# A new order of steps and new shares of casts in the first batch of an attention-and-ReGLU kernel

## The chip, the cores and the metric

The kernel runs on one core of one Trainium2 chip. The metric is the device time of one execution in microseconds (us). The kernel before took 243.38 us (median of 3 runs, 243.06 to 243.96).

## What is computed

Four batches of 12,416 rows of width 128 go through two attention steps against 32 inducing vectors, and the result goes through a ReGLU block of hidden width 1536. Cut to what matters:

```python
def mab(q, kv):
    s = scale * (q @ kv.transpose(0, 2, 1))
    s = s - s.max(-1, keepdims=True)
    a = np.exp(s)
    a /= a.sum(-1, keepdims=True) + 1e-09
    return a @ kv
h = mab(I, x)            # 32 x 128 for each batch, from all 12416 rows of x
y = mab(x, h)            # 12416 x 128 for each batch
gate = np.maximum(y @ w_gate, 0.0)
out = (gate * (y @ w_val)) @ w_out     # 49664 x 128
```

Only 32 values of attention stand between `h` and the output, so that the ReGLU of a row is a quadratic form in these 32 weights; the kernel turns the weights `w_gate`, `w_val` and `w_out` together with `h` into small tables for each batch (the "tables" below) and never forms the 1536-wide product for a row.

## The kernel before

The work of a batch has two stages. The first makes `h`: x is cast to fp16, transposed, multiplied with the inducing vectors (scores), the exponential is taken, and sums over all rows are collected in PSUM. The second makes the gates and tables from `h`, and then the outputs of the batch in blocks of 16 tiles of 128 rows. The second stage of batch 0 and all of batches 1 to 3 stand in one interleaved program that a long text, `ORDER`, spells out step by step. It is not touched.

The first stage of batch 0 has a function of its own, `first_batch`, in which the order is a text too, `HEAD`. The 97 tiles of 128 rows of the batch come in 16 parts, numbered 0 to 15: parts 0 to 9 have 8 tiles each except part 3, which is the one tile left over; parts 10 to 15 have 4 tiles. One DMA for each part is issued on SP (L288), the parts in their order, into four fp32 buffers (parts 0 to 2, 4 to 6, 7 to 9 and 10 to 15), and after them the two weight matrices (L330, L331). A word in `HEAD` is a letter for a step and the number of a part:

- `P`, `A`, `D`: cast of a share of the part's tiles from fp32 to fp16, on POOL, ACT and DVE (L374). `SHARES` says how many tiles each of the three engines takes. The tiles of a part go to POOL first, then to ACT, then to DVE.
- `t`: transposes on PE, one for each tile, into a PSUM bank (L384); `c`: copy of the bank to `xT` on DVE (L388).
- `s`: scores on PE (L394); `e`: exponential on ACT (L400); `h`: the sums on PE (L410 or L421 for the denominators, L425 for the numerators).
- `r0`: a reduction on DVE of the denominators of all 8-tile parts; it is added in front of the last part's sums (L419).

Each engine executes its own words strictly in the order of the text, so a word that is placed early in `HEAD` and has to wait holds up all that follows on its engine. Scores and transposes share a ring of three PSUM banks (tag `g`), in the order of the text too; the exponentials share four buffers.

Behind the last word, POOL casts `w_gate` (L445), issues the load of `w_out` (L446) and the loads of batch 1's x, which cast to fp16 on the way (`x16q`, L236, six of 16 tiles and one of the tile left over). ACT casts `w_val` (L447). PE runs three idle matmuls (`idle`, L357: their result is not read). DVE takes the reciprocal of the denominators (L452), makes `h` (L454) and its centred copies (`centre`, L245 to L266).

`ORDER` begins there: PE makes the gates (L881) and the first scores of the second stage (L511), DVE reads the gates (`gm`, L895, and what follows it), ACT takes the exponential `p` (L520). The buffers of this stage lie where the buffers of the first stage were, so `gm` waits, beside the gates, for the casts of both weights. Two further places matter below: the transposes of batch 1's x on PE (L763), which wait for the `x16q` loads, and the differences on PE (L567), which feed ACT and DVE. Some idle matmuls stand in `ORDER` as well (L1179).

The first stage has further idle matmuls (L357): one in front of the transposes of part 1 and one in front of those of part 2, and three in front of those of part 12, the thirteenth part.

Of the kernel before, what the change touches and what calls it, by code (L numbers as in the profile page):

```python
# [16 lines left out]
class Plan:  # L17
# [68 lines left out]
    (4, 4, 0),  # L86
    (4, 4, 0),
    (4, 4, 0),
    (2, 2, 0),
    (0, 2, 2),  # L90
    (2, 1, 1),
    (2, 2, 0),
    (1, 1, 2),
    (2, 2, 0),
]
HEAD = """
A0 P0 t0 P1 c0 A1 t1 P2 c1 D3 P4 A2 s0 t2 P5 P6 c2 e0 t3 A4 s1 c3 h0 s3 e1 s2 h1 A5 t4 P7 e3 e2
t5 h2 A6 A7 c4 s4 P8 h3 P9 t6 c5 t7 e4 s5 A8 h4 P10 c6 e5 c7 s6 s7 e6 t8 A9 h5 t9 e7 A10 t10
P12 c8 c9 c10 D11 s8 h6 e8 h7 s10 D12 A11 e10 s9 A12 P13 t11 c11 h8 P14 e9 t12 s11 A13 c12 e11
h10 t13 D14 s12 h11 c13 P15 A14 t14 h9 c14 e12 s13 r0 A15 t15 e13 s14 c15 e14 h12 h13 s15 h14  # L100
e15 h15"""

ORDER = """
Ov00LQ0Lu4OV4M24LG4Ow2Oy25k0La000050Or04Oz03Lk0P0020U0Mw0A+0MC0Ox2011Os2Ou2Ot2O-106001000u0524s0P42
# [63 lines left out]
def square_body(ctx, tc, x, inducing, moe_w_gate, moe_w_val, moe_w_out, out):  # L168
# [99 lines left out]
    def first_batch(sp, psum):  # L268
        def bank(tag, name, shape=None, dtype=FP32):
            return psum.tile(  # L270
                shape or [P, BLK], dtype, tag=tag, bufs={"g": 3, "v": 2, "o": 1}[tag], name=name
            )
# [48 lines left out]
        xT = {q: xTq[q] if q < NQ else xTr[0] for q in range(NQ + 1)}  # L321
        hT_ps = bank("o", "hT_ps", [P, M])
        z1a_ps = bank("v", "z1a_ps", [P, 2 * BLK])
        z1a, idle_ps = z1a_ps[:, 0 : 8 * M], z1a_ps[:, BLK : 2 * BLK]
# [28 lines left out]
        n_big = sum(t1 - t0 in (8, 1) for t0, t1 in parts)  # L353

        def idle(ps, n, rhs):
            for _ in range(n):
                nc.tensor.matmul(ps[:, 0 : rhs.shape[-1]], eye16, rhs, start=True, stop=True)  # L357

        def turn(j):
            t0, t1 = parts[j]  # L360
            ps = bank("g", "xT_ps", [P, 8, P], FP16)
            for t in range(t0, t1):
                nc.tensor.transpose(ps[:, t - t0, :], x16[:, t, :], eye16)
            nc.vector.tensor_copy(out=xTs(xT, t0, t1 - t0), in_=ps[:, 0 : t1 - t0, :])

        def part(j):
            return (*parts[j], x32s[j], x16[:, parts[j][0] : parts[j][1], :])
# [8 lines left out]
        def turn(j):  # L376
            t0, t1, _, _ = part(j)
            if j in (1, 2):
                idle(idle_ps, 1, warm)
            if j == n_big + 2:  # L380
                idle(idle_ps, 3, xT[0][:, 0:4, :].rearrange("p t c -> p (t c)"))
            banks[j] = bank("g", "xT_ps", [P, 8, P], FP16)
            for t in range(t0, t1):
                nc.tensor.transpose(banks[j][:, t - t0, :], x16[:, t, :], eye16)  # L384
# [55 lines left out]
        banks, summed = {}, []  # L440
        does = {k: lambda j, e=e: cast(j, e) for e, k in enumerate("PAD")}
        does |= {"t": turn, "c": turned, "s": score, "e": weigh, "h": sums, "r": reduce}
        for word in HEAD.split():
            does[word[0]](int(word[1:]))
# [222 lines left out]
    for Q in range(B * NQ + 1):  # L667
# [9 lines left out]
        ms, mz, p, pp = ("m", "s2", Q), ("m", "z", Q), ("p", Q), ("pp", Q)  # L677
# [729 lines left out]
```

## Time and profile before

| | |
|---|---|
| three timed runs, median (lowest to highest) | 243.38 us (243.06 to 243.96) |
| the profiled execution | 243.17 us |
| its span in the profile | 241.0 us |
| PE busy | 225.6 us (94%) |
| DVE busy | 204.9 us (85%) |
| ACT busy | 204.9 us (85%) |
| POOL busy | 130.2 us (54%) |

The span runs from the first to the last instruction that the profile shows; 2.17 us of the execution lie around it. A row of the timeline has: start in us, time in us, engine, line of the kernel, operation, what it writes and reads with shapes, how many instructions it stands for, and in square brackets how long the engine had been idle before it and what ended that. "q" behind an engine is its queue, which issues DMAs. The end of a matmul is modelled and includes its way through the array; the start of the next row is the better mark for when PE was free.

### The profile page before, as it was taken

The page shows a single profiled execution, that of the slowest core. Times are in us where ns is not written, and L with a number is a line of the kernel's source. Part 1 is how long each engine was busy: PE and PEld are TensorE (multiplying, and loading weights), DVE is VectorE, ACT ScalarE, POOL GpSimd, SP SyncE. Part 2 cuts the span into 40 slices and gives each one's busy share as a digit, 9 for nine tenths or more (in the row PEclk, how much of TensorE's full clock was granted, in tenths as well). Part 3 has the DMA queues.
Part 4 walks back from the last instruction along what each step waited for, and adds up shares of the span by engine and source line. Part 5 has one row for each costly group of instructions (what it writes and reads, how often), then busy time and mean ns, then how long its engine had stood idle before and what let it go on. Part 6 is the DMA issues. An engine that isn't in the chain of part 4 may idle for free.

```text
span 241.0 us, 9825 instructions
## 1 busy us (share of the span) xinstructions
PE 225.6 (94%) x4196; PEld 175.4 (73%) x4196; DVE 204.9 (85%) x444; ACT 204.9 (85%) x376; POOL 130.2 (54%) x164
## 2 busy tenths in 40 slices
PE   5989789999989999999899999999999999999991
PEld 1878357778867888877678787767777777777880
DVE  3665899877999898789999987899998999989892
ACT  3655899979988988998999999899999999998840
POOL 3536706676433439586624356385434886687500
PEclk9999999999999999999999999999999999999999
DMA  6997999999999996999999999355244020647563
GB/s 240 411 392 282 127 212 211 162 188 244 199 220 170 281 245 232 296 173 187 173 226 230 205 187 379 126 224 221 82 172 182 4 90 4 261 177 312 213 265 139
DMA packets 39664, 50.27 MB, mean 209 GB/s; under 512 B 28320, under 2 KB 28992, under 8 KB 39616
## 3 DMA queue, kind: packets, MB, share of 16 engines
q1 hardware_dynamic: 34992, 39.66, 55.8%
q0 software_dynamic: 4576, 9.93, 23.6%
q8 instruction: 33, 0.54, 0.9%
q14 instruction: 15, 0.12, 0.2%
q10 hardware_dynamic: 48, 0.02, 0.0%
HBM read 27.80 MB, written 25.43 MB: 221 GB/s over the span
## 4 chain that ended last, share of the span: by engine, by line
PE 57%; DMA 21%; DVE 10%; ACT 7%; issue 3%; POOL 1%; SPq 0%; DVEq 0%; ACTq 0%; POOLq 0%
PE mb L617 26%; DMA x16q<-in_x_dram 11%; DMA x<-in_x_dram 6%; PE dd L567 5%; PE mb L567 4%; PE mb L1001 4%; DMA w<-in_moe_w_val_dram 4%; PE mb L606 3%; ACT F L581 3%; DVE osb L647 3%; PE mb L793 3%; PE mb L779 3%; PE mb L511 2%; PE mb L763 2%; ACT F L593 2%
## 5 line engine op out<-in xcount | busy, mean ns | idle before, releaser
L581 ACT ACTIVATE F<-dd 128x1024 f16<-128x1024 f32 x97 | 100.6, 1037 | 8.2 <-PE dd L567 4.7
L617 PE MATMUL mb<-T,F 128*128 128x128 f16 x1536 | 105.3, 219 | 0.0
L617 PEld LDWEIGHTS <-F 128*128 128x128 f16 x1536 | 86.7, 98 | 16.4 <-issue 14.9
L593 ACT ACTIVATE F<-mb 128x512 f16<-128x512 f32 x119 | 70.3, 613 | 4.2 <-PE mb L567 3.0
L599 POOL TENSOR_TENSOR F<-F 128x512 f16<-128x512 f16 x57 | 58.4, 1041 | 23.9 <-DVE F L599 8.0
L647 DVE TENSOR_TENSOR osb<-mb,zr 128x512 f32<-128x512 f32 x97 | 64.9, 682 | 5.9 <-PE mb L617 3.0
L595 DVE CAST F<-mb 128x512 f16<-128x512 f32 x75 | 50.3, 684 | 10.7 <-PE mb L567 6.5
L567 PE MATMUL mb<-p,diff 32*128 32x512 f16 (+1 forms) x200 | 39.4, 376 | 0.3 <-DVE ga L899 0.3
L567 PE MATMUL dd<-p,diff 32*128 32x512 f16 (+1 forms) x200 | 37.9, 376 | 1.5 <-ACT F L581 0.9
L530 POOL TENSOR_TENSOR pp<-p 128x512 f16<-128x512 f16 (+1 forms) x22 | 22.2, 1011 | 16.8 <-ACT p L520 5.2
L567 PEld LDWEIGHTS <-diff 32*128 32x128 f16 x400 | 13.3, 91 | 12.0 <-issue 4.5
L606 PE MATMUL mb<-L,pp 32*128 32x128 f16 x384 | 19.4, 215 | 0.3 <-DVE gdev L910 0.2
L1001 PE MATMUL mb<-wo,U 128*128 128x128 f16 x252 | 17.4, 219 | 0.1
L606 PEld LDWEIGHTS <-pp 32*128 32x128 f16 x384 | 12.5, 92 | 6.5 <-issue 2.7
L1001 PEld LDWEIGHTS <-U 128*128 128x128 f16 x252 | 14.6, 98 | 2.2 <-issue 1.6
L520 ACT ACTIVATE p<-mb 128x512 f16<-128x512 f32 (+1 forms) x25 | 14.9, 598 | 1.4 <-DVE gm L895 0.7
L996 POOL TENSOR_TENSOR U<-U,U 128x1536 f16<-128x1536 f16 x3 | 9.3, 3097 | 9.0 <-DVE U L996 9.0
L388 DVE COPY xT<-xT_ps 128x1024 f16<-128x1024 f16 (+1 forms) x15 | 8.6, 581 | 5.5 <-PE xT_ps L384 5.5
L374 POOL CAST x16f<-x 128x512 f16<-128x512 f32 (+2 forms) x14 | 7.5, 539 | 10.6 <-DMA x<-in_x_dram 10.6
L374 ACT CAST x16f<-x 128x512 f16<-128x512 f32 (+2 forms) x15 | 7.7, 515 | 5.6 <-DMA x<-in_x_dram 5.5
L784 ACT ACTIVATE p<-mb 128x512 f16<-128x512 f32 (+1 forms) x21 | 11.6, 561 | 0.7 <-ACT p L520 0.7
L236 POOL DMA_DIRECT2D x16q<-in_x_dram x18 | 10.1, 568 | 2.9 <-PE mb L798 2.9
(161 smaller groups left out, 316.1 us busy)
## 6 DMA issues: line engine op xcount, KB each, us to landing
out_dram<-osb SPq DMA_DIRECT2D x48, 512.0 KB, 4.5
x16q<-in_x_dram POOLq DMA_DIRECT2D x18, 512.0 KB, 9.1
x<-in_x_dram SPq DMA_DIRECT2D x9, 512.0 KB, 6.8
x<-in_x_dram SPq DMA_DIRECT2D x6, 256.0 KB, 9.1
w<-in_moe_w_gate_dram SPq DMA_DIRECT2D x1, 768.0 KB, 8.2
w<-in_moe_w_val_dram SPq DMA_DIRECT2D x1, 768.0 KB, 9.1
wo<-in_moe_w_out_dram POOLq DMA_DIRECT2D x1, 384.0 KB, 5.9
out_dram<-osb SPq DMA_DIRECT2D x1, 256.0 KB, 2.3
```

Source lines behind the costliest of these rows:

```text
L374: f(out=dst[:, a:b, :], in_=x32[:, a:b, :])
L520: act.activation(out=pb[slot["p", Q]][:, 0:w], in_=mb[slot["m", "s2", Q]][:, 0:w], func=AF.Exp, scale=sm_scale / HS,)
L530: engines[e].tensor_tensor(out=p2b[slot["pp", Q]][:, 0:w], in0=a, in1=a, op=ALU.mult)
L567: nc.tensor.matmul(bs[r][:, o], diff[rows, 4 * jj : 4 * jj + 4, :].rearrange("p k m -> p (k m)"), pb[slot["p", Q]][rows, 0:w], start=True, ...
L581: act.activation(out=Fb[slot["F", Q, j]][:, pair(j), :], in_=dd, func=AF.Square, accum_out=None if k is None else spread(Q, k),)
L593: act.activation(out=dst, in_=src, func=AF.Square, **more)
L595: dve.tensor_copy(out=dst, in_=src)
L599: engines[e].tensor_tensor(out=a, in0=a, in1=a, op=ALU.mult)
L606: nc.tensor.matmul(mb[slot["m", "o", Q, r]][:, t * P : (t + 1) * P], p2b[slot["pp", Q]][rows, t * P : (t + 1) * P], L[(Q // NQ) % 2][rows, :],
L617: nc.tensor.matmul(ps[:, t * P : (t + 1) * P], Fb[slot["F", Q, j]][:, r, t * P : (t + 1) * P], T[Q // NQ][:, j, :], start=False, stop=(t, ...
L647: dve.tensor_tensor(out=o[:, 4 * (r % 2) : 4 * (r % 2) + 4, :], in0=mb[slot["m", "o", Q, r]].rearrange("p (t c) -> p t c", t=4), in1=rz.un ...
L1001: nc.tensor.matmul(ps, U[i][:, t, 4 * j : 4 * j + 4, :].rearrange("p k m -> p (k m)"), wo[:, t, :], start=(i, t) == (0, 0), stop=(i, t) == ...
```

## The change

Three things change, all in the first stage of batch 0. The words of `HEAD` come in another order. The shares of casts of parts 10 to 15 are others: the four tiles go to POOL, ACT and DVE as 0/3/1, 2/2/0, 1/0/3, 3/1/0, 3/1/0 and 2/1/1, where they went as 2/2/0, 0/2/2, 2/1/1, 2/2/0, 1/1/2 and 2/2/0. And the three idle matmuls in front of part 12's transposes are gone. Behind line 380 the line numbers of the changed kernel are lower by 3. The loads, `ORDER` and all else stay as they were.

```diff
@@ SHARES, HEAD @@
     (4, 4, 0),
     (4, 4, 0),
     (4, 4, 0),
+    (0, 3, 1),
     (2, 2, 0),
-    (0, 2, 2),
+    (1, 0, 3),
+    (3, 1, 0),
+    (3, 1, 0),
     (2, 1, 1),
-    (2, 2, 0),
-    (1, 1, 2),
-    (2, 2, 0),
 ]
 HEAD = """
-A0 P0 t0 P1 c0 A1 t1 P2 c1 D3 P4 A2 s0 t2 P5 P6 c2 e0 t3 A4 s1 c3 h0 s3 e1 s2 h1 A5 t4 P7 e3 e2
...
-P12 c8 c9 c10 D11 s8 h6 e8 h7 s10 D12 A11 e10 s9 A12 P13 t11 c11 h8 P14 e9 t12 s11 A13 c12 e11
-h10 t13 D14 s12 h11 c13 P15 A14 t14 h9 c14 e12 s13 r0 A15 t15 e13 s14 c15 e14 h12 h13 s15 h14
-e15 h15"""
+P1 A1 A2 t1 P2 c1 t2 c2 A4 P4 s2 A0 e2 s1 P0 t4 D3 e1 t3 c3 c4 h2 t0 P6 P5 h1 s4 A5 P7 A6 e4 A7 t6
...
+c9 h7 P12 A11 P13 t10 h3 s9 h8 c10 P14 e9 D12 t11 A13 c11 s10 t12 h9 e10 s11 A14 t13 c12 s12 r0
+e11 h10 c13 t14 D15 e12 c14 h11 A15 P15 s13 t15 s14 e13 h12 c15 h13 s15 e14 e15 h14 h15"""
@@ turn @@
             if j in (1, 2):
                 idle(idle_ps, 1, warm)
-            if j == n_big + 2:
-                idle(idle_ps, 3, xT[0][:, 0:4, :].rearrange("p t c -> p (t c)"))
             banks[j] = bank("g", "xT_ps", [P, 8, P], FP16)
```

On ACT, the start of the program before (`x16f` is the cast x; `x_124` holds parts 0 to 2, `x_164` parts 4 to 6, `x_168` parts 7 to 9; `p1a` is the exponential):

```order
L374 CAST x16f<-x_124 128x512 x3
L400 ACTIVATE p1a<-s_ps 128x256
L374 CAST x16f<-x_164 128x512
L400 ACTIVATE p1a<-s_ps 128x256
L374 CAST x16f<-x_164 128x512
L400 ACTIVATE p1a<-s_ps 128x32
```

and the same place of ACT in the changed kernel:

```order
L373 CAST x16f<-x_124 128x512 x2
L373 CAST x16f<-x_164 128x512
L373 CAST x16f<-x_124 128x512
L397 ACTIVATE p1a<-s_ps 128x256 x2
L373 CAST x16f<-x_164 128x512 x2
L397 ACTIVATE p1a<-s_ps 128x256
```

ACT now casts parts 1, 2 and 4 first and part 0 behind them; the exponentials come in the order of parts 2, 1, 4, where it was 0, 1, 3.

On DVE, the end of the first stage before (`x_172` holds parts 10 to 15, `xT_96` and `xT_97` are transposed x, `z1s` is the reduction `r0`):

```order
L374 CAST x16f<-x_172 128x256
L374 CAST x16f<-x_172 128x128
L388 COPY xT_96<-xT_ps 128x512
L388 COPY xT_97<-xT_ps 128x512
L374 CAST x16f<-x_172 128x256
L388 COPY xT_97<-xT_ps 128x512 x2
L435 TENSOR_REDUCE z1s<-z1a_ps 128x32
L388 COPY xT_97<-xT_ps 128x512
L452 RECIPROCAL rzs<-z_ps 128x32
```

and there in the changed kernel:

```order
L385 COPY xT_96<-xT_ps 128x512
L373 CAST x16f<-x_172 128x384
L385 COPY xT_96<-xT_ps 128x512
L385 COPY xT_97<-xT_ps 128x512
L432 TENSOR_REDUCE z1s<-z1a_ps 128x32
L385 COPY xT_97<-xT_ps 128x512
L373 CAST x16f<-x_172 128x128
L385 COPY xT_97<-xT_ps 128x512 x2
L449 RECIPROCAL rzs<-z_ps 128x32
```

The reduction has moved ahead of three copies, where one copy stood behind it, and the last part has a DVE cast of its own.

On POOL, from the casts of parts 10 to 15 on, before (`w_0_179` is `w_gate` in fp32):

```order
L374 CAST x16f<-x_172 128x256 x3
L374 CAST x16f<-x_172 128x128
L374 CAST x16f<-x_172 128x256
L445 CAST wg<-w_0_179 128x1536
L446 DMA wo<-in_moe_w_out_dram 128x12x128
L236 DMA x16q_106<-in_x_dram 128x2048
L236 DMA x16q_107<-in_x_dram 128x2048
```

and in the changed kernel:

```order
L373 CAST x16f<-x_172 128x256
L373 CAST x16f<-x_172 128x128
L373 CAST x16f<-x_172 128x384 x2
L373 CAST x16f<-x_172 128x256
L442 CAST wg<-w_0_179 128x1536
L443 DMA wo<-in_moe_w_out_dram 128x12x128
L235 DMA x16q_106<-in_x_dram 128x2048
L235 DMA x16q_107<-in_x_dram 128x2048
```

The shares of the parts are others, the last cast is that of two tiles of part 15 as before, and what stands behind it is the same.

More of the change, by code (lines that the diff above doesn't have):

```diff
@@ L88 @@
     (4, 4, 0),
+    (0, 3, 1),
     (2, 2, 0),
-    (0, 2, 2),
+    (1, 0, 3),
+    (3, 1, 0),
+    (3, 1, 0),
     (2, 1, 1),
-    (2, 2, 0),
-    (1, 1, 2),
-    (2, 2, 0),
 ]
 HEAD = """
-A0 P0 t0 P1 c0 A1 t1 P2 c1 D3 P4 A2 s0 t2 P5 P6 c2 e0 t3 A4 s1 c3 h0 s3 e1 s2 h1 A5 t4 P7 e3 e2
-t5 h2 A6 A7 c4 s4 P8 h3 P9 t6 c5 t7 e4 s5 A8 h4 P10 c6 e5 c7 s6 s7 e6 t8 A9 h5 t9 e7 A10 t10
-P12 c8 c9 c10 D11 s8 h6 e8 h7 s10 D12 A11 e10 s9 A12 P13 t11 c11 h8 P14 e9 t12 s11 A13 c12 e11
-h10 t13 D14 s12 h11 c13 P15 A14 t14 h9 c14 e12 s13 r0 A15 t15 e13 s14 c15 e14 h12 h13 s15 h14
-e15 h15"""
+P1 A1 A2 t1 P2 c1 t2 c2 A4 P4 s2 A0 e2 s1 P0 t4 D3 e1 t3 c3 c4 h2 t0 P6 P5 h1 s4 A5 P7 A6 e4 A7 t6
+c0 s0 t5 e0 c6 h4 s6 t7 h0 c5 e6 P8 A8 s5 P9 h6 s3 c7 P11 t8 e5 c8 e3 s7 A9 h5 t9 e7 D10 s8 A10 e8
+c9 h7 P12 A11 P13 t10 h3 s9 h8 c10 P14 e9 D12 t11 A13 c11 s10 t12 h9 e10 s11 A14 t13 c12 s12 r0
+e11 h10 c13 t14 D15 e12 c14 h11 A15 P15 s13 t15 s14 e13 h12 c15 h13 s15 e14 e15 h14 h15"""
 ORDER = """
```

## The prediction

> **What bounds the kernel now.** I read the chain of waits in order of time first, since it says what the first 45 us hang on:
>
> ```profile
> 15.14 9.07 DMA w<-in_moe_w_val_dram
> ...
> 24.24 1.00 ACT wv L447
> 25.24 1.03 POOL x16q L236 x2
> 26.28 14.00 DMA x16q<-in_x_dram
> 40.28 0.05 issue
> 40.33 0.62 PE mb L763 x8
> ```
>
> From 15 to 40.33 us the chain that ends last is almost all loads: w_val, then x of batch 1. The steps of the first stage that the change reorders do not stand in it. From there on the chain is mainly PE. Next come the timelines of the engines, to see how far each is from setting the time. PE, at the places where batch 1's x is transposed:
>
> ```profile
> 35.19 1.07 PE L763 MATMUL mb<-eye,x16q 128*128 128x128 f16 x16 [0.58 <-DMA x16q<-in_x_dram]
> ...
> 40.33 0.62 PE L763 MATMUL mb<-eye,x16q 128*128 128x128 f16 x8 [0.27 <-DMA x16q<-in_x_dram]
> ```
>
> PE was ready 0.58 and 0.27 us before the x that it needs had landed. ACT and DVE at the same time:
>
> ```profile
> 41.35 0.60 ACT L593 ACTIVATE F<-mb 128x512 f16<-128x512 f32 x1 [0.56 <-PE mb L567]
> ```
>
> ```profile
> 41.39 0.69 DVE L595 CAST F<-mb 128x512 f16<-128x512 f32 x1 [0.25 <-PE mb L567]
> ```
>
> Both wait for the differences that PE makes right behind the late transposes. So at 41 us all three busy engines wait for one load, and whoever is earlier only waits longer. The slack is what they had to spare: 0.27 us on PE, 0.56 on ACT, 0.25 on DVE. POOL shows what starts these loads:
>
> ```profile
> 20.19 0.40 POOL L374 CAST x16f<-x 128x256 f16<-128x256 f32 x1 [0.37 <-DMA x<-in_x_dram]
> 22.07 1.47 POOL L445 CAST wg<-w 128x1536 f16<-128x1536 f32 x1 [1.48 <-DMA w<-in_moe_w_gate_dram]
> 23.48 1.22 POOL L446 DMA_DIRECT2D wo<-in_moe_w_out_dram  x1
> 24.69 3.20 POOL L236 DMA_DIRECT2D x16q<-in_x_dram  x6
> ```
>
> POOL ends its last cast of x at 20.19 + 0.40 = 20.59, then stands idle 1.48 us until w_gate has landed. The x16q loads follow that landing, not the first stage.
>
> **The change: how much earlier the first stage ends.** PE at its end:
>
> ```profile
> 10.95 1.05 PE L384 MATMUL xT_ps<-eye,x16f 128*128 128x128 f16 x16
> 11.84 0.27 PE L410 MATMUL z1a_ps<-p1a,ones 128*128 128x256 f16 x1
> ...
> 17.35 0.40 PE L384 MATMUL xT_ps<-eye,x16f 128*128 128x128 f16 x4 [0.88 <-POOL x16f L374]
> 17.59 0.35 PE L394 MATMUL s_ps<-indT,xT 128*128 128x32 f16 x8
> 17.79 0.27 PE L410 MATMUL z1a_ps<-p1a,ones 128*128 128x256 f16 x1
> ...
> 18.41 0.45 PE L394 MATMUL s_ps<-indT,xT 128*128 128x32 f16 x12
> ...
> 19.32 0.81 PE L357 MATMUL z1a_ps<-xT,eye 128*128 128x512 f16 x3
> 19.96 0.39 PE L384 MATMUL xT_ps<-eye,x16f 128*128 128x128 f16 x4
> ...
> 21.82 0.38 PE L384 MATMUL xT_ps<-eye,x16f 128*128 128x128 f16 x4
> ...
> 23.69 0.81 PE L357 MATMUL z1a_ps<-xT,eye 128*128 128x512 f16 x3
> ```
>
> The last part's cast is done at 20.59, but PE transposes that part at 21.82: PE is 21.82 − 20.59 = 1.23 us behind. From these transposes to the end of the sums (the start of the closing idle matmuls) it takes 23.69 − 21.82 = 1.87 us.
>
> - The three idle matmuls in front of part 12 go: 19.96 − 19.32 = 0.64 us of PE.
> - Before, the scores of part 8 and the sums of parts 6 and 7 stood behind part 10's transposes: 18.41 − 17.59 = 0.82 us. In the new text s8, h6 and h7 stand ahead of t10, inside the 0.88 us for which PE waits for part 10's cast. In their place h3, for one tile, has moved behind t10.
> - Together 0.64 + 0.82 = 1.46 us, more than the 1.23 us by which PE is behind. So the last part can be transposed as soon as it is cast, at about 20.65, and if the tail keeps its 1.87 us the sums end at about 22.5 instead of 23.7: 1.2 us earlier.
>
> Against that stands the new start. ACT and POOL take part 4 ahead of part 0:
>
> ```profile
> 8.77 0.62 POOL L374 CAST x16f<-x 128x512 f16<-128x512 f32 x1 [0.81 <-DMA x<-in_x_dram]
> ```
>
> This is part 4's cast, at its landing; part 0's comes behind it, at about 9.4, where it was the first of all. PE then starts with part 1 at about 6.7, and not with part 0 at 6.1, so some 0.6 us of PE are lost at the front. The price of that is bounded by nothing, if PE catches up in the wait ahead of t10, and the full 0.6 us. I count PE's work ahead of t10 from rows: a part's eight transposes are half of 11.84 − 10.95, 0.45; a part's scores 17.79 − 17.59 = 0.20; its sums half of 18.41 − 17.79, 0.31. Nine parts' transposes and scores and the sums of seven parts are about 9 × 0.65 + 7 × 0.31 = 8.0 us. The slow start adds some 1.4: the transposes of two parts take about twice as long (the two paces are shown below), and an early idle matmul of 0.45 stands between them. From 6.7 that ends at about 16.1, and PE is wanted at 17.35; 1.2 us are left for waits on the way. I take nothing for it. The new casts are of the same 24 tiles; where DVE takes three tiles of part 12, it casts longer than before while PE still has scores and transposes of other parts. I cost them at nothing; the bound is one more DVE cast ahead of the last copies, 0.2 to 0.3 us.
>
> **What the 1.2 us are worth.** The next steps:
>
> ```profile
> 25.20 0.15 DVE L266 CAST hT<-hb 128x1 f16<-128x1 f32 x1
> 26.06 0.17 DVE L895 COPY gm<-mb 128x6 f32<-128x6 f32 x1 [0.72 <-ACT wv L447]
> ```
>
> ```profile
> 24.24 1.47 ACT L447 CAST wv<-w 128x1536 f16<-128x1536 f32 x1 [0.91 <-DMA w<-in_moe_w_val_dram]
> 26.38 0.60 ACT L520 ACTIVATE p<-mb 128x512 f16<-128x512 f32 x1 [0.67 <-DVE gm L895]
> ```
>
> The centred h ends at 25.35, and 1.2 us earlier would be 24.15. The gates on PE would follow, but `gm` waits for the cast of w_val as well. That cast starts when w_val lands, at 24.24, and ends at 24.24 + 1.47 = 25.71. With the few hundredths that a wait takes, `gm` comes at about 25.8: 0.26 us earlier. `p` cannot start before ACT is through with the same cast, so at about 25.85, 0.52 us earlier; the row names `gm` as what it waited for, and if that is so it comes at 26.1, 0.26 us earlier. I take the former for the bound. Of 1.2 us the landing of w_val leaves 0.26 us on DVE and 0.52 on ACT. Then:
>
> ```profile
> 25.00:30.00 5.00, 3.97 (x47) 2.06 (x48) 4.25 (x14) 4.33 (x10) 3.56 (x8) 1.00 1.18 147
> 30.00:35.00 5.00, 4.16 (x55) 2.58 (x52) 5.00 (x8) 5.00 (x11) 0.00 (x0) 1.00 1.06 212
> 35.00:40.00 5.00, 4.80 (x108) 3.81 (x108) 4.88 (x10) 5.00 (x9) 2.27 (x3) 1.00 1.07 212
> ```
>
> The columns are stretch, length, and busy time of PE, its weight loads, DVE, ACT and POOL; then clock, DMA share and GB/s. DVE and ACT are full from 30 to 40, so the 0.26 and 0.52 us are carried to 40 us. There all three wait for the load that lands at 40.28, and the DMA engines have been full all the while (shares of 1.06 to 1.18). POOL's issue of these loads hangs on w_gate's landing and does not move. So PE's wait grows from 0.27 to about 0.5 us, and the sum at 40.33 is **0**. Behind that, nothing is changed. The profiled execution took 243.17 us, 2.17 of them around its span of 241.0, and lies 0.21 below the median of 243.38; I predict **243.2 us**.
>
> [...] The idle matmuls may be there for PE's pace:
>
> ```profile
> 2.42 3.60 PE L311 MATMUL warm_ps<-warm,eye 128*128 128x512 f16 x8 [2.42 <-DVE stackI L300]
> ```
>
> The first eight 512-wide matmuls take 3.60/8 = 0.45 us each; the three at 19.32 come every 0.21. So PE has two paces, and once fast it stays so in this trace: part 12's four transposes take no longer than part 10's. [...] But the new end leaves PE emptier than any stretch before, from the closing idle matmuls to `p`.
>
> **The rivals.**
>
> - *The gain passes.* If x16q lands before compute wants it, in some executions or in all, 0.26 us (DVE) to 0.52 us (ACT) come through: 242.65 to 242.9. For it: PE's slack at 40.33 is only 0.27 us. Against: both waits for x16q name the load. Chance 0.14.
> - *All of it passes*, 1.2 us or more: 242.0 or less. It needs `gm` and the loads of batch 1 not to wait for the weights, against the rows above. Chance 0.05.
> - *The order doesn't do what it is to do*: landings other than these, or ACT and POOL held at part 4, and the stage ends near 23.7 as before. Time as before, 243.2, as long as it ends before 23.69 + 0.25 (DVE's slack). Chance 0.07.
> - *Slower: PE falls back to the slow pace* between the closing idle matmuls and 30 us. From 25 to 30 PE does 3.97 us of work; at half pace it is behind by between 3.97 − 2.5 = 1.47 us and 2.9 us (the same work twice, 7.94, less 5). ACT, fed by it, has 0.56 us to spare at 41.35. So 0.9 to 2.3 us slower, 1.6 in the middle: 244.8. It decides once PE is behind by more than 0.56 us. Chance 0.06.
> - The forecast, absorbed by the load: chance 0.68.
>
> **Range and chances.** The forecast's own width is that of the three runs, 243.06 to 243.96, some 0.5 us to either side. Downward the range takes in the gain that passes (242.65), with some of a run's scatter; upward a stage that ends a few tenths late and the lower part of the slow pace (244.1). That is 242.3 to 244.2, and it leaves out the full gain and most of the slow pace. A measurement of this kernel can tell about 0.5%, 1.2 us, from no change. Faster by more than that is the full gain, 0.06 with scatter; slower by more than that is the slow pace and what I have not seen, 0.06; the rest, 0.88, lies within.
>
> **What would show it.** In the changed kernel's profile the closing idle matmuls of the first stage should start at about 22.5, `gm` at about 25.8 with the cast of w_val as what it waits for, `p` at 25.85 to 26.1, and the transposes near 40.3 with a wait of about 0.5 us for x16q. If `gm` comes earlier than 25.7, the bound by w_val is wrong. If the transposes find x16q there, the loads do not set the time, and the gain would pass. If 512-wide matmuls between 23 and 30 us come every 0.4 us, it is the slow pace. And if the loads of batch 1 land at another time by a microsecond, the total moves with them, whatever the first stage does.

## The result and the profile after

The changed kernel is **slower**: 244.78 us in the median (243.87 to 247.72, 22 runs) against 243.68 us for the kernel before on the same chip (242.65 to 245.38, 22 runs). The ratio is 1.0066 with a 95% interval of 1.0041 to 1.0091, some 1.6 us; the medians lie 1.1 us apart. The prediction was 243.2 us, 242.3 to 244.2, and gave 0.06 to slower. The profiled execution of the changed kernel took 246.91 us with a span of 244.8, one of its longer ones: of the 22 runs 13 lie between 243.9 and 244.9 and 9 between 246.1 and 247.7. A ratio leaves out runs more than 1.5% above the fastest of their kernel; where a kernel's times spread like this, it can differ from that of the medians (e3 below).

I read the changed kernel in the order of the prediction's steps. The row of the page on PE's granted clock comes first; each digit is one fortieth of the span, 6.1 us:

```profile
PEclk9779999999799999999999999999999999999999
```

Two places are below full, where the prediction expected none: the second and third slice, and the eleventh. Next the end of the first stage and the transposes of batch 1's x, from the timelines of PE and DVE in the changed kernel:

```profile
24.46 0.81 PE L356 MATMUL z1a_ps<-xT,eye 128*128 128x512 f16 x3
...
41.16 0.62 PE L760 MATMUL mb<-eye,x16q 128*128 128x128 f16 x8 [0.30 <-DMA x16q<-in_x_dram]
```

```profile
26.84 0.16 DVE L892 COPY gm<-mb 128x6 f32<-128x6 f32 x1 [0.72 <-ACT wv L444]
```

The closing idle matmuls start at 24.46 and not at 22.5, and `gm` and the transposes come 0.78 and 0.83 us later than before. Two things made them late. The loads of this execution landed later: ACT's cast of w_val and POOL's cast of w_gate each start at their landing, and they stood at 24.24 and 22.07 before:

```profile
24.73 1.47 ACT L444 CAST wv<-w 128x1536 f16<-128x1536 f32 x1 [0.57 <-DMA w<-in_moe_w_val_dram]
```

```profile
22.88 1.47 POOL L442 CAST wg<-w 128x1536 f16<-128x1536 f32 x1 [1.47 <-DMA w<-in_moe_w_gate_dram]
```

The transposes wait for the x16q load, which is issued behind w_gate's cast, so their 0.83 us come from the landings. `gm` is another case: w_val's cast, which its row names, ended at 24.73 + 1.47 = 26.20, 0.64 us ahead of it. PE's first gates, before and after, show what it followed:

```profile
25.49 0.38 PE L881 MATMUL mb<-hT,wg 128*128 128x81 f16 x6 [0.99 <-DVE hT L266]
```

```profile
26.27 0.38 PE L878 MATMUL mb<-hT,wg 128*128 128x81 f16 x6 [1.00 <-DVE hT L265]
```

They are 0.78 us later, as `gm` is, and they hang on the end of the first stage, which is 0.77 us later (24.46 against 23.69). In this execution the first stage ends late, and the chain to 41 us goes by the loads all the same. Now the same instruction of the second stage in both kernels, the first matmul of batch 1's tables with `wv`, from PE's timeline before and after:

```profile
68.43 0.31 PE L881 MATMUL mb<-hT,wv 128*128 128x49 f16 x6 [0.47 <-DVE hT L266]
```

```profile
71.84 0.31 PE L878 MATMUL mb<-hT,wv 128*128 128x49 f16 x6 [0.47 <-DVE hT L265]
```

It is 3.41 us later: 2.58 us were lost between 41 and 68 us, in a stretch that the change doesn't touch. The kernel before runs 16 score matmuls there without a break, by its timeline of PE:

```profile
60.68 0.55 PE L779 MATMUL mb<-indT,xT 128*128 128x32 f16 x16
```

The chain of waits of the changed kernel has the same 16 in two pieces:

```profile
61.66 0.06 PE mb L776 x2
61.73 1.18 issue
62.91 0.50 PE mb L776 x14
```

"issue" is time in which PE waits for nothing that the profile shows. Then the windows of the changed kernel around it (columns as in the prediction: busy time of PE, its weight loads, DVE, ACT, POOL; clock, DMA share, GB/s):

```profile
56.00:60.00 4.00, 4.00 (x124) 3.48 (x122) 2.58 (x9) 4.00 (x8) 2.79 (x4) 1.00 0.99 237
60.00:63.40 3.40, 2.22 (x64) 1.63 (x62) 3.20 (x10) 2.59 (x5) 0.53 (x1) 1.00 1.04 184
63.40:67.00 3.60, 3.60 (x55) 3.02 (x54) 0.97 (x3) 2.78 (x6) 1.54 (x4) 0.53 1.04 205
```

PE stands still for 1.2 us, and behind that its clock is at half for 3.41 us (63.45 to 66.86 in the trace's record of the clock; 0.53 in the last stretch above); DVE, which PE feeds, does 0.97 us of work in 3.60. The standstill of 1.2 us and the 3.41 us at half clock, which cost 1.7 at most, make up the 2.58 us. What stands behind moves along with it: the span is 3.8 us longer. The last 0.4 us of that come behind the tables and were not traced.

### The profile page after: what moved, and what is told of

It reads as the page before. It is cut to its first block, busy times and chain, and to the rows that moved or that the text cites. A ratio compares the mean times of both kernels' runs of the same rounds, so it can differ in the third digit from the quotient of the medians.

```text
span 244.8 us, 9819 instructions
## 1 busy us (share of the span) xinstructions
PE 227.0 (93%) x4193; PEld 177.0 (72%) x4193; DVE 205.2 (84%) x444; ACT 205.0 (84%) x375; POOL 130.3 (53%) x164
## 4 chain that ended last, share of the span: by engine, by line
PE 62%; DMA 15%; DVE 10%; ACT 7%; issue 4%; POOL 0%; SPq 0%; DVEq 0%; ACTq 0%
PE mb L614 30%; DMA x<-in_x_dram 6%; DMA x16q<-in_x_dram 6%; PE dd L564 5%; PE mb L564 5%; PE mb L998 4%; PE mb L603 4%; DMA w<-in_moe_w_val_dram 4%; DVE osb L644 4%; ACT F L578 3%; PE mb L790 3%; PE mb L776 3%; PE mb L508 2%; ACT F L590 2%; PE mb L760 2%
## 5 line engine op out<-in xcount | busy, mean ns | idle before, releaser
L614 PEld LDWEIGHTS <-F 128*128 128x128 f16 x1536 | 87.6, 98 | 17.1 <-issue 15.6
L564 PE MATMUL mb<-p,diff 32*128 32x512 f16 (+1 forms) x200 | 40.0, 378 | 0.4 <-DVE ga L896 0.3
L373 POOL CAST x16f<-x 128x512 f16<-128x512 f32 (+3 forms) x14 | 7.8, 567 | 11.2 <-DMA x<-in_x_dram 10.9
L373 ACT CAST x16f<-x 128x512 f16<-128x512 f32 (+3 forms) x14 | 7.2, 522 | 5.7 <-DMA x<-in_x_dram 5.7
```

Source lines behind the costliest of these rows:

```text
L373: f(out=dst[:, a:b, :], in_=x32[:, a:b, :])
L564: nc.tensor.matmul(bs[r][:, o], diff[rows, 4 * jj : 4 * jj + 4, :].rearrange("p k m -> p (k m)"), pb[slot["p", Q]][rows, 0:w], start=True, ...
L614: nc.tensor.matmul(ps[:, t * P : (t + 1) * P], Fb[slot["F", Q, j]][:, r, t * P : (t + 1) * P], T[Q // NQ][:, j, :], start=False, stop=(t, ...
```

## The experiments

All kernels are made from the kernel before or from the changed one; each time is compared with runs of the kernel before on the same chip.

### The idle matmuls or the order

The changed kernel with the three idle matmuls back, the kernel before without them, the changed order with part 0 at its front, and the changed kernel once more.

```diff
e1_new_idle: the changed kernel
+            if j == n_big + 2:
+                idle(idle_ps, 3, xT[0][:, 0:4, :].rearrange("p t c -> p (t c)"))
e2_old_noidle: the kernel before
-            if j == n_big + 2:
-                idle(idle_ps, 3, xT[0][:, 0:4, :].rearrange("p t c -> p (t c)"))
e3_new_part0: the changed kernel, P0 A0 t0 c0 taken from their later places
-P1 A1 A2 t1 P2 c1 t2 c2 A4 P4 s2 A0 e2 s1 P0 t4 D3 e1
+P0 A0 t0 P1 A1 c0 A2 t1 P2 c1 t2 c2 A4 P4 s2 e2 s1 t4 D3 e1
```

> The changed kernel with the three idle matmuls put back ahead of the thirteenth part. Theory A (the new order starves TensorE in its first microseconds, so it falls to half clock for two windows in the first stage): still half clock between about 9 and 16 us, still slower than before, about 244.4. Theory B (without the idle matmuls TensorE's program is six instructions shorter, and a fetch of its instructions comes too late near 62 us, which costs about 1.2 us of waiting and a window at half clock behind it): the runs near 246.5 are gone, no wait over 1 us near 62 us. Theory C (it is only the late landing of the loads in the profiled run): same as before, 243.7.

> The kernel before without the three idle matmuls, its order and shares kept. Theory A: full clock in the first stage, no slower than before, about 243.6. Theory B: some 4 in 10 runs two to three microseconds above the rest, with a wait near 62 us. Theory C: 243.7.

> The changed kernel with part 0 taken first again (cast, transposed and copied ahead of part 1), the rest of the new order, the new shares and no idle matmuls. Theory A: TensorE is fed from 6 us on, full clock in the first stage, the closing idle matmuls start about 1 us earlier than in the changed kernel, and the time is no more than before, 243.2 to 243.7, apart from theory B's runs. Theory B: some 4 in 10 runs near 246. Theory C: 243.7.

> The changed kernel once more, to have its trace a second time beside the others on one chip. Theory A: half clock for two windows in the first stage again. Theory B: runs in two groups, near 244.5 and near 246.5; if this trace is of the faster group it has no wait near 62 us. Theory C: with loads that land as early as in the kernel before's trace (first cast of part 1 at 6.0 us), 243.2 to 243.7.

Measured, against 243.89 us before: e1 243.63 us, ratio 0.9975 (0.9947 to 1.0003); e2 245.66 us, 1.0053 (1.0015 to 1.0091); e3 245.69 us, 1.0012 (0.9969 to 1.0056); e4 244.77 us, 1.0026 (0.9989 to 1.0064). The times of e3 and e4 spread as those of the changed kernel did, 242.89 to 247.02 and 243.41 to 246.89, and their intervals hold 1: against before, their times alone show no loss, and the rows have to. The scores near 60 us in PE's timeline of e1, and then of e2:

```profile
60.43 0.55 PE L778 MATMUL mb<-indT,xT 128*128 128x32 f16 x16
```

```profile
60.23 0.20 PE L777 MATMUL mb<-indT,xT 128*128 128x32 f16 x2
61.88 0.50 PE L777 MATMUL mb<-indT,xT 128*128 128x32 f16 x14 [1.44 <-issue]
```

The old order stalls when it loses the three idle matmuls, and the new order doesn't when it has them: the break comes with the missing idle matmuls, not with the order. e4, the changed kernel itself in another execution, says what the order does. Its timelines of PE, ACT and DVE:

```profile
22.75 0.81 PE L356 MATMUL z1a_ps<-xT,eye 128*128 128x512 f16 x3
...
39.95 0.62 PE L760 MATMUL mb<-eye,x16q 128*128 128x128 f16 x8 [0.31 <-DMA x16q<-in_x_dram]
...
60.31 0.20 PE L776 MATMUL mb<-indT,xT 128*128 128x32 f16 x2
61.73 0.50 PE L776 MATMUL mb<-indT,xT 128*128 128x32 f16 x14 [1.22 <-issue]
...
70.74 0.31 PE L878 MATMUL mb<-hT,wv 128*128 128x49 f16 x6 [0.47 <-DVE hT L265]
```

```profile
24.02 1.47 ACT L444 CAST wv<-w 128x1536 f16<-128x1536 f32 x1 [1.57 <-DMA w<-in_moe_w_val_dram]
25.88 0.60 ACT L517 ACTIVATE p<-mb 128x512 f16<-128x512 f32 x1 [0.38 <-DVE gm L892]
```

```profile
25.58 0.16 DVE L892 COPY gm<-mb 128x6 f32<-128x6 f32 x1 [0.75 <-ACT wv L444]
```

Here the first stage ends at 22.75 and the x16q transposes come at 39.95, with nothing late; the kernel loses its time at 60.31 all the same. So theory C, the late landings of the first profile, is not the cause. Theory A gave the first stage a stretch at half clock as its price. That stretch is in the first profile (clock 0.50 from 10 to 15 us) and not in e4; the first stage was late by it in the one and not in the other, and both break at the scores. e3, with part 0 first, breaks as well. Theory B stands: PE's program is shorter by 6 instructions (a weight load and a matmul for each of three; the pages count 4,193 of each, and 4,196 before), and at one place PE stands still for 1.22 us with nothing in the profile that it waits for.

### How many instructions, and where they stand

If the number counts and not the place, idle matmuls at the end of the first stage will do as well as those in front of part 12.

```diff
f1_new_close6, f3_new_close5: the changed kernel
-        idle(idle_ps, 3, xT[0][:, 0:4, :].rearrange("p t c -> p (t c)"))
+        idle(idle_ps, 6, xT[0][:, 0:4, :].rearrange("p t c -> p (t c)"))   (f3: 5)
f2_old_close0, f4_old_close6: the kernel before
-        idle(idle_ps, 3, xT[0][:, 0:4, :].rearrange("p t c -> p (t c)"))
+        idle(idle_ps, 6, xT[0][:, 0:4, :].rearrange("p t c -> p (t c)"))   (f2: none)
```

> The changed kernel with six closing idle matmuls at the end of the first stage instead of three: as many TensorE instructions ahead of the second stage as in the kernel before, but none of them at the thirteenth part. Theory B (the place of the program in the fetched blocks of TensorE's instructions): no wait over 1 us near 60 us, no window at half clock behind it, 243.0 to 243.7. Rival B2 (the three idle matmuls matter where they stood, because they keep TensorE's clock up): the wait near 60 us stays, 244.8.

> The kernel before without its three closing idle matmuls; those at the thirteenth part stay. It is six instructions shorter, as the changed kernel is. Theory B: a wait of 1.3 to 1.7 us near 60 us, 244.8 to 245.7. Rival B2: none, 243.7.

> The changed kernel with five closing idle matmuls: two instructions shorter than the kernel before, four longer than the changed one. Theory B says only that the wait near 60 us depends on the shift; if the fetch is asked for when a fixed instruction of the program is reached, the wait starts somewhere between a shift of 0 and of 6, and this run says on which side of 2. Rival B2: 244.8.

> The kernel before with six closing idle matmuls: six instructions longer. Theory B: no wait near 60 us, or an earlier one elsewhere; time as before apart from 0.6 us more of idle matmuls that stand beside other waits, 243.7. Rival B2: 243.7.

Measured, against 243.73 us before: f1, as long as before, 243.29 us, ratio 0.9987 (0.9964 to 1.0010); f2, shorter by 6, 246.13 us, 1.0067 (1.0028 to 1.0105); f3, shorter by 2, 246.29 us, 1.0086 (1.0057 to 1.0116); f4, longer by 6, 244.21 us, 1.0019 (0.9997 to 1.0041). PE's timeline of f1, and of f3:

```profile
60.45 0.55 PE L776 MATMUL mb<-indT,xT 128*128 128x32 f16 x16
...
68.20 0.31 PE L878 MATMUL mb<-hT,wv 128*128 128x49 f16 x6 [0.47 <-DVE hT L265]
```

```profile
61.69 0.57 PE L776 MATMUL mb<-indT,xT 128*128 128x32 f16 x16 [1.18 <-DVE hz L808]
```

In the profiles, one for each kernel and two of the changed one, every kernel whose PE program is shorter breaks, wherever the matmuls were taken, and none of equal or greater length does; one idle matmul is enough. f2 lies above the 244.8 to 245.7 that was expected of it; its standstill is 1.87 us. f3's row names DVE for the wait, but what it names had long been done; its time is the same gap as in the others. The place of the break says more: where six instructions are missing PE stops behind two of the 16 matmuls, and where two are missing in front of all 16. Two matmuls with their weight loads are the four instructions between the two, so PE stops at the same count of instructions and not at the same work. f2 still has the idle matmuls in front of part 12 and breaks; f1 has none there and doesn't. Where they stood doesn't matter. f1 against e4 gives the price of the break: `hT,wv` at 68.20 and at 70.74, 2.54 us, which agrees with the 2.58 us of the first profile.

### What delays the instructions

The page of the changed kernel lists a queue that brings instructions, which I take for PE's, since 8,386 of the page's 9,819 instructions are those of PE and its weight loads:

```profile
q8 instruction: 33, 0.54, 0.9%
```

0.54 MB in 33 packets are 16 KB each, and the 8,386 instructions are 254 for each packet. The trace's packet records tell when each starts. Beside the break stands the seventh packet (it starts at 58.13 us before and at 60.60 in the changed kernel), which I take for the one that PE needs there; in the six profiles that break, PE stands still for 1.2 to 1.9 us. Taken from the trace for each kernel: the time at which PE passes the record that lies 256 ahead of the break (about one packet's worth; with 254 it would be 0.02 us later, before and in the changed kernel), the start of the seventh packet, how long after, and when PE goes on at the break's place (1985 records of PE and its weight loads from the start; both times of PE are ends of records):

```
kernel                 PE program   256 ahead   packet   after   goes on
before                     0          56.49     58.13    1.64     60.76
e1_new_idle                0          56.23     56.78    0.55     60.50
f1_new_close6              0          56.25     57.40    1.15     60.52
f4_old_close6             +6          56.46     57.73    1.27     60.73
after                     -6          57.41     60.60    3.19     63.01
e4_after_again            -6          56.19     59.28    3.09     61.83
e2_old_noidle             -6          56.11     59.47    3.36     61.98
e3_new_part0              -6          56.64     60.22    3.58     62.62
f2_old_close0             -6          56.80     60.52    3.72     63.10
f3_new_close5             -2          56.20     59.48    3.28     61.80
```

PE reaches the break 4.3 us after the first of these marks, and goes on some 2.5 us after the packet starts. Where the packet starts within 1.7 us it is in time; where it starts 3.1 to 3.7 us after, it isn't. (g0 and g1, of the next section, are as long as before and have 1.18 and 0.68.) From 56 to 61 us POOL issues the first four loads of batch 2's x, 0.5 MB each, and the DMA engines are full (share 0.99 to 1.04 in the windows above). Two kernels make these four loads small. They leave out 15 of the 16 tiles of each load, so what is computed from these tiles is not the result of the program:

```diff
h1_new_less_load: the changed kernel; h2_close6_less_load: f1_new_close6
     def load(b, q, e):
+        if b == 2 and q < 4:
+            t0, t1 = crange(q)
+            nc.gpsimd.dma_start(out=x16q[slot["x16", b, q]][:, 0:1, :], in_=xv[b][:, t0:t0 + 1, :])
+            return
```

> The changed kernel, but the first four loads of batch 2's x (issued on POOL between 56 and 61 us) bring one tile of 16 instead of all 16; what those chunks compute is left out. Open is why the instruction packet that PE needs near 60.3 us comes late. Theory E (it queues behind these loads, with which it shares the DMA engines): with 0.03 MB in place of 0.5 MB each the packet starts within 2 us of the boundary before it, at about 57.5 us, PE does not stand still near 60.3 and no half-clock window follows; the time is 2 us or more under that of the changed kernel in the lower clock, and equal to h2_close6_less_load within 0.3%. Rival F (what delays it lies in PE's own stream, such as where a wait or the block's boundary falls): the packet still starts at about 59.3, PE stands still for 1.2 us at the same instruction, and h1 is about 1 us or more above h2.

> The control: the changed kernel with six closing idle matmuls (PE's program as long as before), with the same four loads cut to one tile of 16. No stall near 60 us by either theory. What the smaller loads are worth by themselves shows against f1_new_close6: PE was not waiting for batch 2's x near 60 to 75 us in that profile, so the time is that of f1 (0.9987 of before) within 0.5%. Theory E: equal to h1 within 0.3%. Rival F: 1 us or more under h1.

Measured, against 243.71 us before: h1 243.30 us, ratio 0.9983 (0.9964 to 1.0003); h2 243.35 us, 0.9981 (0.9958 to 1.0004). The windows of h1:

```profile
56.00:60.00 4.00, 4.00 (x120) 3.37 (x119) 3.12 (x9) 4.00 (x9) 2.44 (x5) 1.00 0.30 34
60.00:63.40 3.40, 3.40 (x91) 2.79 (x88) 3.20 (x9) 3.40 (x8) 0.42 (x2) 1.00 0.13 14
63.40:67.00 3.60, 3.60 (x57) 2.65 (x55) 3.02 (x10) 3.23 (x9) 2.62 (x5) 1.00 0.46 50
```

With the DMA engines at 0.30 and 0.13, the seventh packet of the shortened program starts at 57.29, 0.46 us after the mark at 56.83; PE doesn't break (3.40 busy of 3.40), the clock stays full, and h1 takes the time of h2, 1.5 us under the changed kernel's median of 244.78. Theory E holds and F doesn't: in the programs shorter by 6 the packet starts 3.09 to 3.72 us after the mark with the loads full, and 0.46 us after it with them small. Why the packet of a program that is 2 instructions shorter (f3, 3.28 us) starts 2 us later than that of the old length (f1, 1.15) stays open. The mark and the first packet of the load fall within 0.2 us of one another in all kernels of the table, so that the two might change their order at some queue. The packet records don't bear that out: the load's first packet starts 0.02 us behind the mark in the kernel before and 0.02 ahead of it in f1, which don't break, and 0.12 behind it in e3 and 0.11 ahead of it in f2, which do.

### Where the gain of the first stage goes

The prediction let the load of batch 1's x absorb 1.2 us. If that is so, the load has to come sooner for the gain to show. It is issued behind POOL's cast of w_gate, so DVE takes most of that cast here, in the kernel before (g0) and in f1 (g1).

```diff
-        nc.gpsimd.tensor_copy(out=wg, in_=w32[0])
+        nc.vector.tensor_copy(out=wg[:, 0:1280], in_=w32[0][:, 0:1280])
+        nc.gpsimd.tensor_copy(out=wg[:, 1280:DFF], in_=w32[0][:, 1280:DFF])
```

> The kernel before, with the cast of w_gate split: VectorE takes 1280 of its 1536 columns and GpSimd the last 256. GpSimd is then free about 1.1 us earlier to issue the load of w_out and the loads of batch 1's x. Theory D (the late loads of batch 1's x hide what the first stage gains): these loads land about 1 us earlier, TensorE's wait ahead of the transposes near 40 us is gone, and as much passes as the engines had to spare, 0.25 us: 243.1 to 243.5. Rival D2 (the loads are limited by the DMA engines, not by their issue): they land as before, 243.7.

> The changed kernel with six closing idle matmuls, with the same split of the cast of w_gate. Theory D: the loads land about 1 us earlier and now the earlier end of the first stage passes too, 0.26 us on VectorE beside the 0.25 us that the old order gains: transposes near 39.6 us with no wait for the load, 242.7 to 243.1, the fastest of all. Rival D2: as without the split, 243.3. No wait over 1 us near 60 us in either of the two, since the number of TensorE's instructions is that of the kernel before.

Measured, against 243.68 us before: g0 243.35 us, ratio 0.9979 (0.9957 to 1.0001); g1 **242.80 us**, 0.9957 (0.9937 to 0.9978), faster than both kernels. POOL in g1:

```profile
22.46 1.05 POOL L443 CAST wg<-w 128x256 f16<-128x256 f32 x1 [1.49 <-DMA w<-in_moe_w_gate_dram]
23.46 1.22 POOL L444 DMA_DIRECT2D wo<-in_moe_w_out_dram  x1
24.67 3.19 POOL L235 DMA_DIRECT2D x16q<-in_x_dram  x6
```

and PE's transposes in g0, then in g1:

```profile
39.82 0.62 PE L764 MATMUL mb<-eye,x16q 128*128 128x128 f16 x8
```

```profile
39.45 0.62 PE L761 MATMUL mb<-eye,x16q 128*128 128x128 f16 x8
```

No row names the load any more; PE finds x there. The transposes come at 39.82 and 39.45, where they were at 40.33 before and at 40.09 in f1. From w_gate's landing to the first issue it is 1.92 us in g0 and 2.21 in g1, where it was 2.62 before and in f1: 0.7 and 0.4 us sooner, and not the 1.1 that was expected. The load that the transposes need landed at 39.13 in g0 and 39.26 in g1, 1.15 and 1.02 us sooner than before (40.28). In g0 its issue was 0.66 us sooner. In g1 w_gate had landed 0.39 us later than in the profile of before, and the load was issued no sooner in clock time (26.25 against 26.28); what let it land sooner there stays open. With the load out of the way some of the first stage's gain passes. It ends 0.66 us earlier in g1 than in g0 (23.01 and 23.67); the transposes are 0.37 us apart and the medians 0.55 (242.80 against 243.35; the two intervals overlap, so that the size is not certain).

## Why the prediction was wrong

- **The first stage ends at 22.5**: right but for 0.25 us. It was 22.75 in e4 and 22.79 in e3, 0.94 and 0.90 us earlier than before and not 1.2. The two terms of that sum can be seen apart: without the three idle matmuls the old order ends at 23.18 (e2), and with them the new one at 23.19 (e1), each 0.5 us earlier than 23.69. They were taken for 0.64 and 0.82. It was 24.46 in the profile of the changed kernel, where the loads were late and PE ran at half clock from 8.84 to 15.66 us; that hasn't come back in another execution, and its cause was not tried.
- **The landing of w_val leaves 0.26 us on DVE and 0.26 to 0.52 on ACT**: right. In e4 w_val landed at 24.02; 24.02 + 1.47 + 0.09 = 25.58, where `gm` stands. That is under the 25.7 that was to speak against the bound, but w_val had landed 0.22 us sooner. `p` follows `gm` by 0.30, so the smaller of the two values holds on ACT.
- **The load of x16q absorbs it, sum 0 at 40.33**: right. e4 waits 0.31 us for it at 39.95; 0.5 was forecast, and the load landed 0.38 us sooner than before. It is the step that g0 and g1 tested.
- **"Behind that, nothing is changed"**: this step failed. The removed idle matmuls were priced as 0.64 us of PE and no more; with 6 instructions less the seventh packet of instructions also starts 3.09 us after its mark (e4), where it was 1.64 before, among the loads of x at 60 us. That costs 1.2 us of standing still and, with the half clock behind it, 2.5 us in each of the profiles compared (2.58 and 2.54), and 1.6 us over all runs by the ratio. In kernels whose PE program has kept its length the new order is at 0.9975 (e1) and 0.9987 (f1) of before: the forecast of no change.
- **The rival of the slow pace** had the right kind of loss and, by luck, the right size (244.8), at the wrong place and from another cause. It saw it between the closing idle matmuls and 30 us. That the emptier PE of that stretch brings the slow pace is not shown: in e4 the clock stayed full there (1.00 from 25 to 30 us), and in h1, the same program up to the loads at 56 us, it fell (0.50). The windows of h1 show what that is worth:

```profile
25.00:30.00 5.00, 5.00 (x43) 2.02 (x43) 3.99 (x10) 4.42 (x9) 3.65 (x8) 0.50 1.18 152
...
35.00:40.00 5.00, 4.54 (x84) 3.61 (x84) 4.91 (x9) 5.00 (x11) 2.15 (x3) 1.00 1.06 208
```

  PE's timeline of h1 at the transposes of batch 1's x, and then that of h2, whose clock is full:

```profile
35.09 1.10 PE L764 MATMUL mb<-eye,x16q 128*128 128x128 f16 x16
...
40.50 0.62 PE L764 MATMUL mb<-eye,x16q 128*128 128x128 f16 x8
```

```profile
35.08 1.07 PE L764 MATMUL mb<-eye,x16q 128*128 128x128 f16 x16 [0.90 <-DMA x16q<-in_x_dram]
...
40.23 0.62 PE L764 MATMUL mb<-eye,x16q 128*128 128x128 f16 x8 [0.29 <-DMA x16q<-in_x_dram]
```

  The half clock costs 0.27 us there, not 0.9 to 2.3, and the medians of h1 and h2 are alike: the waits for the loads, 0.90 and 0.29 us in h2, took the rest. In e2 the clock fell there too, from 25.48 to 28.89 us, and PE reaches the scores at 60.23, no later than in e4 (60.31). Whether the idle matmuls in front of part 12 also hold the clock up is not settled: of the nine profiles without them three have half clock between 8 and 32 us (the first one, e2, h1), of the five with them none.
- **The range** reached to 244.2 and missed the median by 0.6 us. Part of that is the measure: the kernel before is 243.68 in the longer comparison, 0.30 above the three runs on which the prediction stood.

Open is which of the timed runs of the changed kernel have the break. All six profiles of shortened kernels with full loads show it, but their times reach down to 242.9 (e3) and 243.4 (e4), so that some runs have probably less of it or none. The kernel before has a few long runs too (246.56 and 246.97 us), and no profile shows what made these long.

## What to carry to other kernels

Here two instructions less on PE, an engine that is busy for 93 to 94% of the span, were enough to make one 16 KB packet of instructions late: it starts 3.28 us after its mark in f3 and 1.15 in f1, and PE stands still for 1.18 us in f3. After a change that takes instructions from such an engine, look for a gap on it that is released by "issue" in the middle of a group of equal instructions, at a time when the DMA engines are full (0.98 to 1.04 here), and fill the program up to its old length to tell it from the change itself. What the earlier end of a stage is worth hung on the next load here: the new order at the old length took 0.9987 of the time before (f1), and 0.9957 with w_gate's cast split ahead of that load (g1), where the split alone took 0.9979 (g0). Bring the load in sooner first, and then change the order.

## What the hardware showed that was not expected

- With a standstill of PE of 1.2 to 1.9 us comes a stretch at half clock in each of the six profiles that break: 3.41 us in the changed kernel (63.45 to 66.86), and 6.8 us in f2, which stood still longest (1.87 us).
- With the DMA engines full of the program's own loads, a packet of instructions started up to 3.7 us after its mark; with four of these loads cut to a sixteenth it started after 0.46 us.
